# Dividing on GpSimd in slots 4 to 7 and inverting on GpSimd in slots 9 to 23, in a top-k attention kernel with a GELU layer behind it

## The chip, the cores and the metric

One core of a Trainium2 chip runs the whole kernel. It has a matrix engine (TensorE, PE in the profile), a vector engine (VectorE, DVE), an engine for activation functions and copies (ScalarE, ACT), a general engine (GpSimd, POOL), and a queue engine that issues transfers (SyncE, SP). Each works through its own queue of instructions in order, and waits at semaphores for the others. The metric is the device time of one execution in microseconds.

## The reference, cut to what matters

```python
# q, k, v: 8 batches, 8 heads, 576 rows, 64 columns
scores = np.matmul(q, k.transpose(0, 1, 3, 2)) / np.sqrt(64)
kth = np.partition(scores, -32, axis=-1)[..., -32:-31]
scores = np.where(scores >= kth, scores, -1e9)
scores = scores - np.max(scores, axis=-1, keepdims=True)
attn = np.exp(scores)
attn = attn / (np.sum(attn, axis=-1, keepdims=True) + 1e-09)
x = np.matmul(attn, v)        # then (batch, head, row, column) -> 4608 x 512
h = x @ w_in                  # 512 -> 2048
g = h * (1.0 / (1.0 + np.exp(-1.702 * h)))
out = g @ w_out               # 2048 -> 512
```

## The kernel before, in words

The attention is cut into 144 slots. A slot holds 128 rows of query for two heads, or the 64-row ends of two pairs of heads. For each slot the kernel does the following:

- `scores(n)`: TensorE multiplies queries and keys into two banks (`s_ps`). `copy_scores(n)`: ScalarE copies them to a buffer `sc`, of which there are four.
- `pair_up(n)`: VectorE makes the larger and the smaller of each two scores (`ranked`). `topk(n)`: four rounds of MAX8 and three of MATCH_REPLACE8 for each head, on VectorE, give the 32 largest scores (`top`).
- `bounds(n)`: GpSimd makes from them a cut and a bias (`cut`, `low`). `mask(n)` and `exps(n)`: ScalarE drops what is under the cut and takes exponentials (`pr`), with their sums (`den`).
- `invert(n)`: GpSimd adds 1e-9 to the sums (`some`), and VectorE takes the reciprocal (`rden`).
- Then the exponentials are divided by their sums and transposed (`pt`), which goes in two ways. In the first slots, `divide(n)` has GpSimd make two diagonal matrices from `rden`, and `turn_main` and `turn_ends` multiply the exponentials by these on TensorE, which divides and transposes at once; ScalarE copies the result out of the bank. Later, `normalize(n)` divides on GpSimd in place, `split(n)` has ScalarE take the 16-bit halves apart into the buffer `sc` and SyncE write them to memory (`rows`), and `turn_by_dma(n)` brings them back transposed.
- `values`: TensorE multiplies by v, and ScalarE copies the result to its place (`xT`).

Slot n works on the top-k of slot n, and on the exponentials and the division of slot n - 1. The first way is used for the heads of slots 0 to 7, the second from slot 8 on (`BY_DMA = 8`). Besides, in the first slots the weights are loaded and rounded on ScalarE, VectorE and GpSimd (`round_piece`; a shift of each piece is VectorE's). From slot 4 on, TensorE does pieces of the GELU layer (`hidden` and `project`, names `ph`, `unit` and `po`), in each slot and up to the end of the kernel; `tanh` is ScalarE's, `gate` and `combine` are mostly GpSimd's.

What sets the order of the work: slots 0 to 24 (`COLLECTED = 25`) are not issued as they are called. Each step is recorded, and `issue_in_order` issues the steps in the order of the table `ORDER`, which is a list of step numbers; "208+4" means four steps from 208. An engine's queue holds its steps in that order. Slots from 25 on are issued as `joined_pair` writes them, two slots at a time. In the profile, instructions of the table have the line of the recording helper's deferred call, L133, and those of later slots L132.

Of the kernel before, what the change touches and what calls it, by code (L numbers as in the profile page):

```python
# [19 lines left out]
P = 128  # L20
# [125 lines left out]
def kernel(  # L146
# [104 lines left out]


    pieces = [(c, g) for g in range(NG) for c in range(CC)] + [(None, f) for f in range(FC)]
    raw = {}

    def load_piece(n):
        c, g = pieces[n]
# [916 lines left out]
    def slot(n):  # L1174
# [37 lines left out]
        for i, op in enumerate(topk(n)):  # L1212
# [6 lines left out]
            if i == (9 if n < 3 else 7):  # L1219
                if n > BY_DMA:  # L1220
                    invert(n - 1)
                elif n > 0:
                    divide(n - 1)
# [514 lines left out]
```

## Time and profile before

| what | value |
|---|---|
| median of 3 runs | 1342.28 us (1342.17 to 1343.64) |
| the profiled execution | 1342.64 us |
| its span in the profile | 1340.9 us, mean granted TensorE clock 0.996 |
| busy share of the span | PE 99%, PEld 90%, DVE 94%, ACT 86%, POOL 73% |
| DMA | 249.27 MB, mean 186 GB/s |

"Busy" is the time with an instruction of the engine in flight; for PE the ends are modelled, so its share overstates how close it is to its peak. PEld is the loading of the stationary operand, which overlaps with PE. Rows of groups give the busy time, the mean duration of one instruction, and the idle time of the engine before them with what ended it. Rows of the timeline give start and length in microseconds, and in brackets the idle time before, and who ended it. Consecutive instructions of one engine overlap a little in such rows, so the cost of one in a row of them is the distance between starts.

### The profile page before, as it was taken

The numbers are of one execution on the slowest core, as the hardware profiler recorded it, in microseconds if no ns is written. First come the engines' busy times: TensorE is split into PE (matmuls) and PEld (weight loads), VectorE is DVE, ScalarE is ACT, GpSimd is POOL, SyncE is SP. The second block draws the span as 40 slices with busy tenths as digits, with TensorE's granted clock in tenths as the row PEclk, the third lists the DMA queues.
The fourth block names the chain that finished last, engine by engine and source line by source line (L and its number), as shares of the span: only waits on it lengthen the run. The fifth ranks groups of instructions, "written<-read, shape, count | busy, mean of one in ns | idle before, by whom it ended". The sixth has DMA issues, their size and how long they took to land.

```text
span 1340.9 us, 54139 instructions
## 1 busy us (share of the span) xinstructions
PE 1326.5 (99%) x22528; PEld 1202.9 (90%) x22528; DVE 1266.9 (94%) x3371; ACT 1158.4 (86%) x1871; POOL 978.6 (73%) x1788
## 2 busy tenths in 40 slices
PE   8999999999999999999999999999999999999998
PEld 5777689899999999999999999999999999999998
DVE  7999999999999999999999999999999999999902
ACT  6999998999999988999999989899998988888831
POOL 3888987777777777777777777777777777777761
PEclk8999999999999999999999999999999999999999
DMA  7553878888998798989999787988999878755650
GB/s 239 173 169 119 191 182 201 213 191 205 218 219 195 169 206 195 236 191 202 205 220 205 184 188 181 235 199 195 186 228 214 199 158 170 189 140 145 149 116 18
DMA packets 532358, 249.27 MB, mean 186 GB/s; under 512 B 463760, under 2 KB 510352, under 8 KB 532112
## 3 DMA queue, kind: packets, MB, share of 16 engines
q1 hardware_dynamic: 531520, 245.38, 78.5%
q8 instruction: 176, 2.88, 0.9%
q14 instruction: 70, 0.57, 0.1%
q10 hardware_dynamic: 592, 0.43, 0.1%
HBM read 46.01 MB, written 104.60 MB: 112 GB/s over the span
## 4 chain that ended last, share of the span: by engine, by line
PE 94%; DVE 3%; DMA 1%; ACT 1%; SPq 1%; issue 0%; POOL 0%; DVEq 0%; ACTq 0%; POOLq 0%
PE unit L132 32%; PE po L132 29%; PE mixed L132 12%; PE s_ps L132 7%; PE po L133 6%; PE s_ps L133 2%; PE o L133 2%; PE tp L133 2%; PE ph L133 2%; DVE ranked L133 1%; DVE top L133 1%; DMA pt<-rows 1%; ACT sc L133 1%; DMA rows<-sc 0%; SPq L133 0%
## 5 line engine op out<-in xcount | busy, mean ns | idle before, releaser
L132 DVE MAX8 top<-ranked 128x8 f32<-128x288 f32 (+1 forms) x952 | 518.2, 596 | 0.0
L132 PE MATMUL unit<-xT,win 128*64 128x128 f32 x7936 | 454.3, 273 | 0.0
L132 PEld LDWEIGHTS unit<-xT,win 128*64 128x64 f32 x7936 | 437.4, 137 | 0.0
L132 DVE MATCH_REPLACE8 ranked<-top,ranked 128x288 f32<-128x288 f32 x714 | 384.1, 543 | 0.0
L132 PE MATMUL po<-wout,th 128*64 128x128 f32 x4032 | 330.0, 274 | 0.0
L132 POOL TENSOR_TENSOR th<-th,th 128x128 f32<-128x128 f32 x374 | 273.9, 732 | 29.9
L132 PE MATMUL po<-raws,th 128*64 128x128 f32 x3064 | 252.9, 273 | 0.0
L132 PEld LDWEIGHTS po<-wout,th 128*64 128x64 f32 x4032 | 238.3, 137 | 9.9 <-issue 5.1
L132 POOL TENSOR_SCALAR pr<-pr,rden 128x576 f32<-128x576 f32 x240 | 176.5, 745 | 75.2 <-DVE rden L132 75.2
L132 ACT COPY sc<-pr 128x2304 uint16<-128x2304 uint16 x96 | 205.5, 2140 | 1.2 <-POOL pr L132 1.2
L132 PEld LDWEIGHTS po<-raws,th 128*64 128x64 f32 x3064 | 184.6, 137 | 0.0
L132 ACT ACTIVATE th<-unit 128x512 f32<-128x512 f32 x124 | 74.9, 604 | 94.4 <-PE unit L132 94.4
L132 ACT ACTIVATE pr<-sc,low 128x576 f32<-128x576 f32 x192 | 148.1, 786 | 0.0
L132 ACT ACTIVATE sc<-sc,cut 128x576 f32<-128x576 f32 x192 | 140.7, 797 | 0.0
L132 PE MATMUL s_ps<-qk_t 64*64 64x512 f32 x936 | 139.1, 596 | 1.4 <-ACT sc L133 0.8
L132 POOL TENSOR_SCALAR some<-den 128x2 f32<-128x2 f32 x120 | 26.5, 220 | 155.7 <-ACT pr L132 155.4
L132 DVE TENSOR_TENSOR ranked<-s_ps,sc 128x576 f32<-128x576 f32 x188 | 132.8, 748 | 0.0
L132 ACT COPY sc<-s_ps 128x1024 f32<-128x1024 f32 x93 | 95.6, 1028 | 33.8 <-PE s_ps L132 33.7
L132 POOL TENSOR_TENSOR th<-th 128x128 f32<-128x128 f32 x250 | 114.8, 459 | 0.4
L133 DVE MAX8 top<-ranked 128x8 f32<-128x576 f32 (+1 forms) x200 | 111.6, 598 | 0.0
L132 POOL TENSOR_TENSOR raws<-raws 128x128 f32<-128x128 f32 (+1 forms) x160 | 89.7, 569 | 8.1 <-ACT raws L132 3.0
L132 POOL TENSOR_SCALAR th<-th 128x512 f32<-128x512 f32 x124 | 76.5, 617 | 13.1 <-ACT th L132 13.1
(145 smaller groups left out, 2196.6 us busy)
## 6 DMA issues: line engine op xcount, KB each, us to landing
rows<-sc SPq DMA_DIRECT2D x112, 576.0 KB, 3.7
rows<-spare SPq DMA_DIRECT2D x24, 576.0 KB, 3.6
qk_rows<-pr SPq DMA_DIRECT2D x23, 576.0 KB, 4.9
out_dram<-raws SPq DMA_DIRECT2D x66, 128.0 KB, 3.1
raws<-in_moe_w_in_dram SPq DMA_DIRECT2D x16, 512.0 KB, 4.9
raws<-in_moe_w_out_dram SPq DMA_DIRECT2D x16, 512.0 KB, 3.8
qk_l<-in_q_dram SPq DMA_DIRECT2D x28, 256.0 KB, 4.6
qk_l<-in_k_dram SPq DMA_DIRECT2D x28, 256.0 KB, 4.8
```

Of the source, the lines that this page charges most:

```text
L132: return do(*args, **kwargs)
L133: self.engines.collected.append(lambda: do(*args, **kwargs))
```

## The change

Three things change, all in slots 0 to 24.

1. For the heads of slots 4 to 7 the diagonals are no longer made. `slot(n)` calls `invert(n - 1)` in place of `divide(n - 1)` when n is over `TURNS = 4`, and `normalize(n - 1)` divides on GpSimd ahead of `turn_main` and `turn_ends`. Where a slot has no diagonals, `turn` transposes with the identity on TensorE. Eight diagonals leave GpSimd, eight divisions of 128x576 come; on TensorE 32 matmuls with 128 columns and 8 with 64 columns become 36 transposes.
2. In slots 9 to 23 `invert` takes the reciprocal as a power of -1 on GpSimd, from a constant tile that is filled at the start. Fifteen reciprocals leave VectorE. The heads of slots 0 to 8 and those from 24 on keep the reciprocal.
3. The table `ORDER` is new. It is the same up to the step that follows "208+4 130 163 156", and differs from there on to its end. Apart from the steps named above, every engine issues the same instructions as before.

```diff
@@ -37,86 +37,85 @@
 8 11 0+8 9 12 10 13+5 22 18 23+2 33 25 19 26+5 20 31 34 32 21 38+4 35 97 36+2 98 42+8 99 50 54+2 100 56+4 53 51
...
-208+4 130 163 156 213+4 166 157 131 167 159 132 194 191 168 192 212 175 161 171 218 172+3 170 177 158 176 265
...
+208+4 130 163 156 172+3 166 157 131 167 179+3 158 132 171 191 170 213+4 192 194 160 176 212 168 175 178 159 218
...
@@ -252,6 +251,8 @@
     raw = {}
+    minus_one = const.tile([P, 2], F32, name="minus_one")
+    nc.gpsimd.memset(minus_one[:], -1.0)
...
@@ -570,7 +571,10 @@
         rden = st[n]["rden"] = small.tile([P, 2], F32, name="rden", tag="inverse")
-        nc.vector.reciprocal(rden[:], some[:])
+        if BY_DMA < n < COLLECTED - 1:
+            nc.gpsimd.tensor_tensor(out=rden[:], in0=some[:], in1=minus_one[:], op=ALU.pow)
+        else:
+            nc.vector.reciprocal(rden[:], some[:])
...
@@ -595,7 +599,9 @@
             at = (first + c) * P
-            if first != NF:
+            if "by" not in st[n]:
+                nc.tensor.transpose(tp[:, c * P : (c + 1) * P], pr[:, at : at + P], ident[:])
+            elif first != NF:
                 by = st[n]["by"][:, first // NF, :]
...
@@ -1217,7 +1223,7 @@
             if i == (9 if n < 3 else 7):
-                if n > BY_DMA:
+                if n > TURNS:
                     invert(n - 1)
                 elif n > 0:
                     divide(n - 1)
@@ -1249,6 +1255,8 @@
         elif n >= TURNS:
+            if n > TURNS:
+                normalize(n - 1)
             turn_main(n - 1)
             turn_ends(n - 1)
```

157 rows, old and new, of the table ORDER are left out of this document.

## The prediction

> **What bounds the kernel now.** I read the page's first lines, then busy time by stretch, then the chain of waits round the end of slot 24, then VectorE's own idle places. First the page: span, busy time, and the chain that ended last.
>
> ```profile
> span 1340.9 us, 54139 instructions
> PE 1326.5 (99%) x22528; PEld 1202.9 (90%) x22528; DVE 1266.9 (94%) x3371; ACT 1158.4 (86%) x1871; POOL 978.6 (73%) x1788
> PE 94%; DVE 3%; DMA 1%; ACT 1%; SPq 1%; issue 0%; POOL 0%; DVEq 0%; ACTq 0%; POOLq 0%
> ```
>
> TensorE looks like the bound everywhere, but the page itself says that a busy PE is modelled. The change lies in slots 3 to 24, roughly the first 246 us, so I read that part by stretch. Columns: window, length, then busy time of PE, PEld, DVE, ACT, POOL; PEclk; DMA share; GB/s.
>
> ```profile
> 33.00:67.00 34.00, 32.76 (x295) 24.20 (x295) 33.38 (x91) 32.30 (x62) 28.99 (x36) 1.00 0.53 170
> 67.00:110.00 43.00, 42.33 (x365) 31.23 (x360) 41.48 (x110) 40.39 (x82) 36.96 (x50) 1.00 0.44 134
> 110.00:200.00 90.00, 89.86 (x1035) 67.72 (x1029) 89.61 (x239) 87.65 (x146) 80.29 (x114) 1.00 0.71 181
> 200.00:246.00 46.00, 44.58 (x822) 39.68 (x817) 44.89 (x122) 40.97 (x69) 33.83 (x65) 1.00 0.81 194
> 300.00:800.00 500.00, 500.00 (x9080) 466.30 (x9078) 499.34 (x1330) 450.02 (x704) 368.17 (x707) 1.00 0.89 202
> ```
>
> From 33 to 246 us VectorE is idle for 0.62 + 1.52 + 0.39 + 1.11 = 3.64 us in all. Weight loading fills 71 to 87% of those stretches against 93% later, so PE is not at its peak there, while VectorE cannot go faster than its list of top-k steps. The chain at the end of slot 24 agrees (start, length, what):
>
> ```profile
> 244.37 1.85 DVE ranked L132 x4
> 246.22 0.04 issue
> 246.27 1.09 PE s_ps L132 x8
> ...
> 247.57 3.21 PE po L132 x56
> ```
>
> Up to 246 us the last thing waited for is VectorE; from there PE runs without a gap almost to the end (500.00 busy of 500 us). PE's work behind that point is the same in both kernels, so a microsecond that VectorE gains before 246 us is a microsecond off the end, and a microsecond of PE work saved before it is worth something only where VectorE waited for PE.
>
> **The change, part by part.**
>
> *Reciprocals off VectorE, slots 9 to 23.* Fifteen leave. Their recorded 0.15 us overlaps the next instruction, so I take start to start:
>
> ```profile
> 119.41 0.16 DVE L133 RECIPROCAL rden<-some 128x2 f32<-128x2 f32 x1
> 119.49 1.40 DVE L133 MAX8 top<-ranked 128x8 f32<-128x576 f32 x2
> 129.44 0.15 DVE L133 RECIPROCAL rden<-some 128x2 f32<-128x2 f32 x1
> 129.50 0.74 DVE L133 MAX8 top<-ranked 128x8 f32<-128x576 f32 x1
> ```
>
> That is 0.08 and 0.06, so 15 x 0.07 = 1.05 us, all on the bounding engine. VectorE's places of idle time that matter here (in brackets the idle time before, and who ended it):
>
> ```profile
> 81.27 0.76 DVE L133 TENSOR_TENSOR ranked<-s_ps,sc 128x576 f32<-128x576 f32 x1 [0.19 <-PE s_ps L133]
> 101.77 0.76 DVE L133 TENSOR_TENSOR ranked<-s_ps,sc 128x576 f32<-128x576 f32 x1 [0.95 <-PE s_ps L133]
> 110.39 0.76 DVE L133 TENSOR_TENSOR ranked<-s_ps,sc 128x576 f32<-128x576 f32 x1 [0.40 <-PE s_ps L133]
> 225.29 0.17 DVE L133 RECIPROCAL rden<-some 128x2 f32<-128x2 f32 x1 [0.25 <-POOL some L133]
> 227.10 0.76 DVE L133 TENSOR_TENSOR ranked<-s_ps,sc 128x576 f32<-128x576 f32 x1 [0.86 <-ACT sc L133]
> ```
>
> One moved reciprocal stood waiting for GpSimd, in order ahead of top-k steps: 0.25 us, which goes too.
>
> *Plain transposes, heads of slots 4 to 7.* Eight 128-wide matmuls per head become transposes, and two half-wide ones become one.
>
> ```profile
> 103.62 1.95 PE L133 MATMUL tp<-xT,pr 128*128 128x128 f32 x16
> 105.40 0.59 PE L133 MATMUL po<-wout,th 128*128 128x512 f32 x1
> ...
> 148.81 0.60 PE L133 MATMUL tp<-ident,raws 128*128 128x128 f32 x4
> 149.25 1.02 PE L133 MATMUL po<-wout,th 128*128 128x512 f32 x2
> ```
>
> Start to start, eight matmuls (16 records) take 1.78 us and four transposes 0.44, so eight take 0.88: 0.90 saved per head. The block of the ends took this long in the chain:
>
> ```profile
> 106.43 0.37 PE tp L133 x4
> ```
>
> It becomes one transpose of 0.11: up to 0.26 more, and nothing if its two halves already overlap with other work. Four heads: 3.6 to 4.6 us, I take 4.0. PE has slack there, so none of this counts by itself. What counts is the three waits on score matmuls, 0.19 + 0.95 + 0.40 = 1.54 us, in slots 8, 10 and 11, at and behind the heads that are saved. Adding these durations along PE's queue in the two issue orders, the last score matmul of slots 8, 10 and 11 comes 10.4, 2.4 and 4.9 us of PE work earlier in the new one, and those of slots 12 to 24 come 1.3 to 6.0 earlier. I count the 1.54 us as gone; bounds 0 and 1.54.
>
> *GpSimd: what is added.* These are the groups of the first 270 us (xcount | busy, mean ns | idle):
>
> ```profile
> L133 POOL TENSOR_SCALAR pr<-pr,rden 128x576 f32<-128x576 f32 x32 | 23.7, 749 | 4.0 <-DVE rden L133 3.8
> L133 POOL TENSOR_TENSOR th<-th,th 128x512 f32<-128x512 f32 x10 | 12.8, 1278 | 0.2
> L133 POOL TENSOR_SCALAR xT<-ident,rden 128x128 f32<-128x128 f32 x16 | 5.9, 373 | 0.5
> L133 POOL TENSOR_TENSOR low<-cut 128x2 f32<-128x2 f32 x25 | 4.9, 194 | 0.6
> ```
>
> Eight divisions of 0.749 come, eight diagonals of 0.373 go: +3.0 us. GpSimd idles 6.04 us between 67 and 110, so they are covered; the transposes now wait 0.75 us longer per head for their data, and behind them in PE's queue stand the score matmuls, whose lead pays it. Fifteen powers come, an operation that no row shows. Its bounds are the 128x2 tensor_tensor (0.194) and the 128x512 one (1.28): 2.9 to 19.2 us in all. It has the small one's shape, so I take 0.19. GpSimd idles 9.71 + 12.17 = 21.9 us between 110 and 246, so either end is hidden in the sum. On the path of one slot the power replaces a wait of 3.8 / 7 = 0.54 us (the division's row above: seven waits for the reciprocal), so it breaks even there at 0.54. The memset of the constant is one small instruction at the start: nothing, since GpSimd waits there for the first top-k.
>
> *The new table.* It keeps the sequence of the first 170 or so steps and changes the rest. Added along the queues with the same durations, the pairings of VectorE lie up to 2.8 us later among its own steps, and the ScalarE copies that they need move by similar amounts, so that their lead changes by under a microsecond in most slots; it shrinks by 0.8 in slot 24, where VectorE waits already (0.86 above). Bounds: the idle time of VectorE left over from the two items above, 3.64 - 1.54 - 0.25 = 1.85 us, may go entirely, or one more wait as long as a scores-buffer transfer may come (4.57 us, below). I take no change.
>
> *What hides the rest, and what comes next.* ScalarE must follow VectorE. At the end of slot 24 its sums come late:
>
> ```profile
> 247.31 0.22 POOL L132 TENSOR_SCALAR some<-den 128x2 f32<-128x2 f32 x1 [3.08 <-ACT pr L132]
> ...
> 248.17 0.16 DVE L132 RECIPROCAL rden<-some 128x2 f32<-128x2 f32 x1
> ```
>
> This reciprocal stays on VectorE, with a lead of 248.17 - 247.53 = 0.64 us. If VectorE comes 2.84 us earlier and ScalarE doesn't, VectorE waits 2.2 us here. For ScalarE's coming along speak 5.03 idle us of it between 200 and 246, and that its waits in the opening are mostly for PE, which now leads by 4 us:
>
> ```profile
> ACT pt L133 <- PE tp L133: 2.6, 6, 0.8
> ACT xT L133 <- PE o L133: 2.2, 4, 1.6
> ```
>
> *Sum.* 1.05 + 0.25 + 1.54 = 2.84 us. The profiled execution took 1342.64 us, 1.7 more than its span and 0.36 more than the median of 1342.28; the difference carries over, so 1342.28 - 2.84 = **1339.4 us**.
>
> [...] In the stretch of 110 to 200 us, which holds the transposes quoted at 148.81, the granted clock is 1.00. [...] I give it 0.04.
>
> **Rivals.**
>
> *ScalarE sets the pace instead.* Place: the reciprocal at 248.17. VectorE keeps the 0.64 us of lead, the rest is waited away: 1342.28 - 0.64 = 1341.6. For it: ScalarE's 87.65 of 90 us busy from 110 to 200. Against: its waits for PE. Chance 0.21.
>
> *The power is dear: slower.* Place: GpSimd's queue from slot 10 on, where the division of the same head and the bounds of the next slots stand behind it. It decides from 21.9 / 15 = 1.46 us each. At 2 us it adds 15 x 0.54 = 8.1 us beyond GpSimd's idle time, and PE's waits are off: 1342.28 - 2.84 + 8.1 = 1347.5. For it: no row shows a power on GpSimd. Against: two elements per partition, and 0.19 for a sum of that size. Chance 0.12. [...]
>
> *The table brings one more wait for a buffer.* The pairing at 227.10 waited for this chain:
>
> ```profile
> 221.76 4.57 DMA rows<-sc
> ...
> 226.43 0.65 ACT sc L133
> ...
> 227.10 1.19 DVE ranked L133 x2
> ```
>
> A copy of scores needs the buffer whose transfer out is still running. One such full wait more: 1339.4 + 4.57 = 1344.0; two: 1348.5. For it: slot 24's lead shrinks. Against: divisions no longer wait for VectorE. Chance 0.14.
>
> **How the numbers follow.** Forecast 0.49, between 1337.6 (all 3.64 us of idle and the 1.05 go) and 1340.5 (half of PE's waits and the 0.25 stay); ScalarE 0.21; power 0.12; buffer 0.14; clock 0.04. The range leaves out the power and the case of two buffer waits, and reaches a little past both ends that are left: 1337.3 to 1345.0. Changes of 0.2%, 2.7 us, are about what a measurement of this kernel can tell from none. Faster than that, below 1339.6: five sixths of the forecast, 0.41. Slower, above 1345.0: the power, and half of the buffer case (more than one full wait): 0.19. Within: 0.40.
>
> **What would show it.** In the changed profile: VectorE's pairings of slots 8, 10 and 11 without a PE wait; eight transposes near 0.9 us per head; powers near 0.2 us; the chain handing over from VectorE to PE near 243.4 us instead of 246.27, with PE full behind it. Wrong would be: powers above 1.4 us, VectorE waiting for sums near the end of slot 24, new waits on copies of scores in slots 13 to 24, or a clock below 1.00 between 67 and 110 us.

## The result, and the profile after

The change made the kernel slower: 1345.50 us (1344.99 to 1348.61) against 1342.62 us (1341.62 to 1343.85) beside it, medians of 11 runs each, a ratio of 1.0021 with a 95% interval of 1.0013 to 1.0028. It is 2.9 us more, where 2.8 us less were forecast. The profiled execution took 1347.45 us, 2 us above that median, so its own difference to the profile of before (4.8 us) is larger than the typical one. Of these 4.8 us 0.97 are there at VectorE's first pairing (10.23 us against 9.26), where both kernels still issue the same order; in four kernels of the experiments, which have that order up to there too (`old_pow`, `old_both`, `new_none`, `old_plain`), that pairing begins at 9.34 to 9.92 us. At least a part of that share, then, is not the change's.

First the page of the changed kernel: span, busy time, and the engines in the chain that ended last. (Here the table's instructions have line L132 and those of later slots L131; in the kernels of the experiments these lines shift by a few.)

```profile
span 1345.7 us, 54053 instructions
PE 1327.3 (99%) x22484; PEld 1202.2 (89%) x22484; DVE 1268.6 (94%) x3356; ACT 1158.6 (86%) x1871; POOL 993.5 (74%) x1804
PE 82%; DMA 1%; ACT 0%; SPq 0%; issue 0%; DVE 0%; DVEq 0%
```

VectorE's 3% of the chain have gone to 0%: it is no longer VectorE that ends the table's part. The same stretches as before (busy PE, PEld, DVE, ACT, POOL, then the granted clock, DMA share, GB/s):

```profile
33.00:67.00 34.00, 29.72 (x239) 21.97 (x238) 32.68 (x88) 29.32 (x57) 28.04 (x38) 0.89 0.49 164
67.00:110.00 43.00, 41.78 (x332) 28.86 (x330) 41.74 (x109) 40.43 (x81) 36.97 (x46) 1.00 0.40 127
110.00:200.00 90.00, 90.00 (x970) 66.09 (x970) 89.60 (x234) 87.82 (x152) 85.08 (x121) 1.00 0.70 180
200.00:246.00 46.00, 44.62 (x846) 40.23 (x846) 44.23 (x112) 40.55 (x64) 42.29 (x76) 1.00 0.84 189
300.00:800.00 500.00, 499.47 (x9068) 465.53 (x9066) 498.70 (x1327) 449.75 (x704) 367.53 (x706) 1.00 0.90 201
```

Three things are to be seen. From 33 to 67 us, ahead of nearly all that was edited, TensorE is busy for 29.72 us instead of 32.76, at a mean clock of 0.89 instead of 1.00. From 110 to 246 us GpSimd has 13.3 us more to do (127.37 against 114.12). And the steady part from 300 us on is what it was. The first of these, in TensorE's timeline (in brackets the idle time before, and who ended it):

```profile
37.41 0.70 PE L132 MATMUL s_ps<-qk_t 64*64 64x288 f32 x2 [1.42 <-DVE ranked L132]
...
46.22 1.39 PE L132 MATMUL tp<-xT,pr 128*128 128x128 f32 x8 [2.10 <-POOL xT L132]
```

TensorE stands 2.10 us for the diagonals of an early head. In GpSimd's timeline these diagonals come behind 2.55 us of weight pieces that the new table puts ahead of them:

```profile
43.11 2.55 POOL L132 TENSOR_TENSOR win<-win,raws 128x512 int32<-128x512 int32 x2
45.61 0.20 POOL L132 TENSOR_TENSOR low<-cut 128x2 f32<-128x2 f32 x1
45.79 0.73 POOL L132 TENSOR_SCALAR xT<-ident,rden 128x128 f32<-128x128 f32 x2
```

Behind that gap the granted clock is 0.50 for six microseconds:

```profile
44.00:47.00 3.00, 0.90 (x9) 0.79 (x8) 2.97 (x10) 3.00 (x5) 3.00 (x6) 1.00 0.74 265
47.00:53.00 6.00, 5.55 (x32) 4.73 (x34) 6.00 (x17) 4.73 (x11) 4.29 (x5) 0.50 0.48 155
```

GpSimd's groups of the first 270 us (xcount | busy, mean ns | idle):

```profile
L132 POOL TENSOR_SCALAR pr<-pr,rden 128x576 f32<-128x576 f32 x40 | 29.9, 752 | 0.9 <-PE tp L132 0.3
...
L132 POOL TENSOR_TENSOR rden<-some,minus_one 128x2 f32<-128x2 f32 x15 | 11.0, 736 | 0.2
...
L132 POOL TENSOR_TENSOR low<-cut 128x2 f32<-128x2 f32 x25 | 5.5, 219 | 0.4
```

A power of two elements per partition takes 0.736 us on average, not 0.19. Then VectorE's waits from 90 us on:

```profile
94.77 0.76 DVE L132 TENSOR_TENSOR ranked<-s_ps,sc 128x576 f32<-128x576 f32 x1 [0.65 <-ACT sc L132]
125.66 1.42 DVE L132 TENSOR_TENSOR ranked<-s_ps,sc 128x576 f32<-128x576 f32 x2 [0.40 <-ACT sc L132]
...
223.70 0.76 DVE L132 TENSOR_TENSOR ranked<-s_ps,sc 128x576 f32<-128x576 f32 x1 [0.36 <-ACT sc L132]
232.42 0.76 DVE L132 TENSOR_TENSOR ranked<-s_ps,sc 128x576 f32<-128x576 f32 x1 [0.72 <-ACT sc L132]
243.70 1.42 DVE L132 TENSOR_TENSOR ranked<-s_ps,sc 128x576 f32<-128x576 f32 x2 [0.56 <-ACT sc L132]
```

No pairing waits for TensorE's score matmuls any more, as forecast; they wait for ScalarE's copies (`sc`) instead, which stood among the prediction's signs of being wrong. Last the chain of waits where the table's part ends (start, length, what):

```profile
216.49 3.85 DMA rows<-sc
220.33 0.02 issue
220.35 9.38 DMA pt<-rows
229.73 0.14 issue
229.86 2.60 PE o L132 x80
...
248.61 1.53 PE po L132 x28
...
252.25 2.76 PE po L131 x47
```

TensorE takes over from a transfer at 229.86 and works without a gap through the point that was 247.57 before and is 252.25 now. Of the 4.8 us 4.7 are there by then. What comes last ahead of that stretch is no longer VectorE, but two transfers behind a copy of ScalarE's.

### The profile page after: what moved, and what is told of

The parts are those of the page before. It is cut to its first block, busy times and chain, and to the rows that moved or that the text cites. A ratio compares the mean times of both kernels' runs of the same rounds, so it can differ in the third digit from the quotient of the medians.

```text
span 1345.7 us, 54053 instructions
## 1 busy us (share of the span) xinstructions
PE 1327.3 (99%) x22484; PEld 1202.2 (89%) x22484; DVE 1268.6 (94%) x3356; ACT 1158.6 (86%) x1871; POOL 993.5 (74%) x1804
## 4 chain that ended last, share of the span: by engine, by line
PE 82%; DMA 1%; ACT 0%; SPq 0%; issue 0%; DVE 0%; DVEq 0%
PE unit L131 32%; PE po L131 29%; PE mixed L131 12%; PE s_ps L131 7%; DMA pt<-rows 1%; PE ph L132 1%; PE po L132 0%; PE o L132 0%; DMA rows<-sc 0%; ACT sc L132 0%; PE s_ps L132 0%; SPq L131 0%; DVE raws L131 0%; ACT pr L132 0%; ACT th L131 0%
## 5 line engine op out<-in xcount | busy, mean ns | idle before, releaser
L131 DVE MAX8 top<-ranked 128x8 f32<-128x288 f32 (+1 forms) x952 | 518.5, 597 | 0.0
L131 PE MATMUL unit<-xT,win 128*64 128x128 f32 x7936 | 454.2, 273 | 0.0
L131 PEld LDWEIGHTS unit<-xT,win 128*64 128x64 f32 x7936 | 437.4, 137 | 0.0
L131 DVE MATCH_REPLACE8 ranked<-top,ranked 128x288 f32<-128x288 f32 x714 | 384.5, 544 | 0.0
L131 PE MATMUL po<-wout,th 128*64 128x128 f32 x4032 | 329.8, 274 | 0.0
L131 POOL TENSOR_TENSOR th<-th,th 128x128 f32<-128x128 f32 x374 | 274.3, 733 | 29.9
L131 PE MATMUL po<-raws,th 128*64 128x128 f32 x3064 | 252.8, 273 | 0.0
L131 PEld LDWEIGHTS po<-wout,th 128*64 128x64 f32 x4032 | 238.1, 137 | 9.9 <-issue 5.3
L131 POOL TENSOR_SCALAR pr<-pr,rden 128x576 f32<-128x576 f32 x240 | 177.3, 750 | 74.0 <-DVE rden L131 74.0
L131 ACT COPY sc<-pr 128x2304 uint16<-128x2304 uint16 x96 | 205.5, 2141 | 1.0 <-POOL pr L131 0.9
L131 PEld LDWEIGHTS po<-raws,th 128*64 128x64 f32 x3064 | 184.5, 137 | 0.0
L131 ACT ACTIVATE th<-unit 128x512 f32<-128x512 f32 x124 | 74.9, 604 | 94.5 <-PE unit L131 94.5
L131 ACT ACTIVATE pr<-sc,low 128x576 f32<-128x576 f32 x192 | 148.1, 786 | 0.0
L131 POOL TENSOR_SCALAR some<-den 128x2 f32<-128x2 f32 x120 | 26.6, 222 | 157.0 <-ACT pr L131 156.4
L131 ACT ACTIVATE sc<-sc,cut 128x576 f32<-128x576 f32 x192 | 140.8, 797 | 0.1
L131 PE MATMUL s_ps<-qk_t 64*64 64x512 f32 x936 | 139.0, 596 | 0.0
L131 DVE TENSOR_TENSOR ranked<-s_ps,sc 128x576 f32<-128x576 f32 x188 | 132.8, 749 | 0.4 <-ACT sc L132 0.4
L131 ACT COPY sc<-s_ps 128x1024 f32<-128x1024 f32 x93 | 95.6, 1028 | 33.8 <-PE s_ps L131 33.7
L131 POOL TENSOR_TENSOR th<-th 128x128 f32<-128x128 f32 x250 | 115.1, 460 | 0.4
L132 DVE MAX8 top<-ranked 128x8 f32<-128x288 f32 (+1 forms) x200 | 111.0, 595 | 0.0
L131 POOL TENSOR_TENSOR raws<-raws 128x128 f32<-128x128 f32 (+1 forms) x160 | 89.9, 571 | 8.1 <-ACT raws L131 3.0
L131 POOL TENSOR_SCALAR th<-th 128x512 f32<-128x512 f32 x124 | 77.4, 624 | 13.1 <-ACT th L131 13.1
```

The lines of the kernel that those rows point to most:

```text
L131: return do(*args, **kwargs)
L132: self.engines.collected.append(lambda: do(*args, **kwargs))
```

## The experiments

The change has three parts: the powers, the divisions with plain transposes, and the table. Four kernels were made first, to take them apart. A table for a program that lacks an edit is the other table's sequence, with the steps that the edit replaces standing where their replacements stood. The theories: T, the table itself is the loss; P, the power is; L, the later transposes are (they wait for divisions instead of diagonals). The kernels ran in several rounds, on three chips, and the median of before lay between 1342.62 and 1344.74 us; so each kernel is compared with the runs of before beside it, by a ratio with its 95% interval, and two kernels by the difference of their ratios (0.0010 is 1.34 us).

*The new table alone* (`new_none`): the code of before, with the order of the changed kernel.

> The new table alone, without either edit: each reciprocal stands on VectorE at the place of its power, each diagonal at the place of a division, and the second half of a block of ends right behind the first. Theory T (the table is the loss, through waits in slots 2 to 9): 3 to 5 us slower than before, with the VectorE waits for copies of scores in the first 100 us as in the changed kernel. Theory P (the power is the loss): within 1 us of before. Theory L (the later transposes are the loss): within 1 us of before.

Measured: 1349.70 us, ratio 1.0037 [1.0023, 1.0051]. Without either edit the new order costs 5 us, as theory T had it. TensorE's gap of 2.10 us stands there too, and so does the fall of the clock behind it, with no plain transpose in the program:

```profile
45.80 1.44 PE L127 MATMUL tp<-xT,pr 128*128 128x128 f32 x6 [2.10 <-POOL xT L127]
```

```profile
43.00:46.00 3.00, 0.90 (x11) 0.39 (x4) 3.00 (x7) 3.00 (x4) 3.00 (x5) 1.00 0.75 248
46.00:50.00 4.00, 3.55 (x21) 2.96 (x21) 3.97 (x13) 2.76 (x7) 2.43 (x4) 0.57 0.61 213
```

*The powers alone, in the old order* (`old_pow`):

```diff
-        nc.vector.reciprocal(rden[:], some[:])
+        if BY_DMA < n < COLLECTED - 1:
+            nc.gpsimd.tensor_tensor(out=rden[:], in0=some[:], in1=minus_one[:], op=ALU.pow)
+        else:
+            nc.vector.reciprocal(rden[:], some[:])
```

> The power alone with the old table. Theory T: 0 to 1.3 us faster than before. Theory P (0.72 us each on GpSimd, 10.8 us in all, hold up the divisions and the bounds behind them): 2 to 4 us slower. Theory L: 0 to 1.3 us faster.

Measured: 1348.06 us, ratio 1.0025 [1.0016, 1.0034], 3.3 us slower. In its profile everything stands within 0.1 us of before until slot 11; then VectorE falls behind, 1.3 us by slot 15 and 3.8 by slot 24, in waits such as these:

```profile
168.75 0.76 DVE L128 TENSOR_TENSOR ranked<-s_ps,sc 128x576 f32<-128x576 f32 x1 [1.00 <-ACT sc L128]
...
230.89 0.76 DVE L128 TENSOR_TENSOR ranked<-s_ps,sc 128x576 f32<-128x576 f32 x1 [1.82 <-ACT sc L128]
```

ScalarE's copies come late because ScalarE stands waiting at an earlier step of its queue. Its waits between 110 and 246 us (us in total, times, longest), before and with the powers:

```profile
ACT sc L133 <- POOL pr L133: 1.4, 4, 0.6
```

```profile
ACT sc L128 <- POOL pr L128: 5.3, 9, 1.2
```

`split` copies the divided exponentials, the division stands behind the power on GpSimd, and the next slot's score copy stands behind `split` on ScalarE. So ScalarE waited for a division nine times in this stretch, against four before, although GpSimd was idle for 13.3 of its 136 us.

*The divisions and plain transposes alone, in the old order* (`old_plain`):

```diff
-                if n > BY_DMA:
+                if n > TURNS:
                     invert(n - 1)
...
+            if n > TURNS:
+                normalize(n - 1)
```

> Divisions and plain transposes in slots 5 to 8 alone, with the old table. Theory T: 0 to 2 us faster than before. Theory P: 0 to 2 us faster. Theory L (the transposes wait for the divisions): 2 to 4 us slower.

Measured: 1344.95 us, ratio 1.0005 [0.9993, 1.0017]. Four microseconds less of TensorE's work bring nothing that can be told in the old order. In three of its twelve runs the mean granted clock is under 0.995, which none of the 29 runs of before beside it shows, and these three took 1346.9 to 1350.2 us. The profiled execution is one of them: the shorter transposes leave a longer gap (0.68 us before), and behind it the clock falls.

```profile
73.21 1.15 PE L128 MATMUL tp<-ident,pr 128*128 128x128 f32 x8
75.75 0.43 PE L128 MATMUL o<-pt,v_l 128*64 128x128 f32 x2 [1.39 <-ACT pt L128]
```

```profile
77.00:83.00 6.00, 6.00 (x26) 4.25 (x25) 5.50 (x15) 6.00 (x14) 5.76 (x6) 0.51 0.98 248
```

*Both edits, in the old order* (`old_both`): the two diffs above together.

> Both edits with the old table: each power at the place of its reciprocal, each division at the place of a diagonal. Theory T: 1 to 3 us faster than before (the 1.05 us of reciprocals and part of the 1.54 us of waits for PE, less what the longer steps on GpSimd cost). Theory P: 2 to 4 us slower. Theory L: 2 to 4 us slower.

Measured: 1348.44 us, ratio 1.0032 [1.0020, 1.0043]. So the new order, which costs 5 us by itself, takes some 1.5 us back once both edits are there (1.0021 against 1.0032; the intervals overlap). L falls: by `old_plain` the later transposes cost nothing that can be told. T and P hold in part, and the parts don't add up. The next kernels were for that.

*The new order with divisions and transposes, without powers* (`new_plain`): the changed kernel with `nc.vector.reciprocal(rden[:], some[:])` in all slots.

> The changed kernel with its table, its divisions and its plain transposes; the fifteen inversions go back to VectorE as reciprocals, at the places that the powers have in the table. If the power of 0.72 us on GpSimd still costs in the new table what it costs in the old one (3.3 us for the powers alone), this is 2 to 3 us faster than the changed kernel: ratio to before 0.9995 to 1.0005. If the new table hides the powers, the fifteen reciprocals (1.05 us) come back for nothing and the waits for GpSimd with them: ratio 1.0020 to 1.0035. With the diagonals too the new table alone took 1.0037; the plain transposes in it should then be worth 1 to 2 us.

*The changed kernel with a product in place of the power* (`new_times`), *and the old order with that product* (`old_times`); both leave out the inversion, and keep all else:

```diff
-            nc.gpsimd.tensor_tensor(out=rden[:], in0=some[:], in1=minus_one[:], op=ALU.pow)
+            nc.gpsimd.tensor_tensor(out=rden[:], in0=some[:], in1=minus_one[:], op=ALU.mult)
```

> The changed kernel with the power replaced by a product of the same two tiles on GpSimd (128x2, the inverse is left out, so that the division multiplies by minus the sum). It should take the 0.19 to 0.22 us that I had put down for the power, and all else, the order too, is the changed kernel's. If the mis-sized power is a loss of the changed kernel: 1.5 to 3 us faster than it, ratio to before 0.9995 to 1.0010. If the new table hides the power's length: within 0.5 us of the changed kernel, ratio 1.0018 to 1.0025.

> The old table with the inversions of slots 9 to 23 on GpSimd as a product (the inverse is left out) in place of the power; diagonals and matmuls as before. If the 3.3 us that the powers alone cost in the old table come from their length of 0.72 us, this one is before less 1.05 (reciprocals) and less up to 0.25 (one wait): ratio 0.9990 to 0.9995. If they come from the place in GpSimd's queue and not from the length, the ratio stays at 1.0020 to 1.0025.

Measured: `new_plain` 1346.29 us, ratio 1.0017 [1.0008, 1.0025]; `new_times` 1346.61, 1.0018 [1.0009, 1.0027]; `old_times` 1344.59, 1.0006 [0.9998, 1.0015]. The product took what I had put down for the power:

```profile
L128 POOL TENSOR_TENSOR rden<-some,minus_one 128x2 f32<-128x2 f32 x15 | 2.9, 196 | 0.5
```

In the old order the power's length is 2.6 of its 3.3 us (1.0025 against 1.0006). In the changed kernel it is worth 0.4 us, within the intervals: with the plain transposes there, the new order hides most of it. `new_plain` fell between its two ranges, and `old_times` missed both of its own. It is the change as I had priced it, fifteen reciprocals off VectorE for 0.2 us each on GpSimd, and it isn't faster than before. Its VectorE waits show where the 1.05 us went:

```profile
174.89 0.76 DVE L128 TENSOR_TENSOR ranked<-s_ps,sc 128x576 f32<-128x576 f32 x1 [0.32 <-ACT sc L128]
...
228.41 0.76 DVE L128 TENSOR_TENSOR ranked<-s_ps,sc 128x576 f32<-128x576 f32 x1 [1.62 <-ACT sc L128]
258.71 0.17 DVE L127 RECIPROCAL rden<-some 128x2 f32<-128x2 f32 x1 [0.45 <-POOL some L127]
```

Before, the wait at the same pairing was 0.86 us (227.10), and the other two were none. In the trace of before, ScalarE's copies end 0.16 to 0.92 us ahead of VectorE's pairing in ten of the slots 12 to 23; here five of these have no lead left. VectorE ran into them. ScalarE's own waits for divisions hardly grew (1.8 us in all, against 1.4 before), which speaks for ScalarE's pace, and against the move to GpSimd, as what took the gain.

*Old order first, new order behind* (`old_then_new`): both edits; the old order up to VectorE's first step of slot 9 (the seam), then the remaining steps in the new one.

> Both edits; the steps stand in the old table's order up to VectorE's first step of slot 9, and in the new table's order behind it. If the new table's loss lies in slots 2 to 8 (in the profiles VectorE falls 2.8 us behind in slots 3 to 6, and 3.2 by slot 9, the later start aside), this is about 3 us faster than the changed kernel: ratio to before 0.9990 to 1.0005. If the loss comes from the order behind slot 9, or is made good there by the early order, the ratio is 1.0020 or more.

Measured: 1345.43 us, ratio 1.0016 [1.0006, 1.0027]. It fell between its two ranges and didn't tell: the old order brought its gap of 1.41 us behind the plain transposes of 73 us along, and the clock fell there, as in `old_plain` (0.50 from 78 to 83 us), and once more behind a gap of 2.12 us that ends at 99.67 (0.50 from 101 to 104). So the seam was moved ahead of these transposes.

*The same with the seam at slot 5* (`early_old5`), *and the changed kernel on the same chip* (`after_again`).

> Both edits; the steps stand in the old table's order up to VectorE's first step of slot 5 and in the new table's order behind it. Theory G (the new table lets TensorE idle 2.10 us at 44 us, behind GpSimd's late diagonals, and the granted clock falls to half for some 4 to 7 us): with the old order there the gap is 0.81 us as before, the clock stays at 1.00 from 33 us on, and the kernel is 2 to 3 us faster than the changed one: ratio to before 0.9993 to 1.0005. Rival B (the loss lies behind slot 9, where ScalarE has no lead on VectorE): ratio 1.0015 or more. With the new order behind slot 5 the gap of 1.4 us at 74 us that the old order had together with plain transposes should not be there either.

> The changed kernel once more, on the same chip as the three others, as their base: ratio 1.0013 to 1.0028 as measured, a gap of TensorE of about 2.1 us near 44 us and a clock of 0.5 for some microseconds behind it in the profile.

Measured: `early_old5` 1344.81 us, 1.0015 [1.0006, 1.0024]; `after_again` 1346.00, 1.0022 [1.0013, 1.0031]. The gap at 44 us and the low clock are gone with the old order, but the time lies where rival B had put it (1.0015 or more), and not where theory G had (at most 1.0005):

```profile
33.00:67.00 34.00, 30.10 (x245) 21.24 (x244) 33.93 (x91) 31.08 (x60) 30.66 (x39) 1.00 0.51 165
67.00:110.00 43.00, 42.53 (x351) 29.55 (x353) 42.10 (x109) 40.50 (x82) 36.85 (x45) 1.00 0.44 134
110.00:200.00 90.00, 90.00 (x986) 66.07 (x983) 89.60 (x235) 86.93 (x148) 85.70 (x123) 1.00 0.68 177
200.00:246.00 46.00, 46.00 (x870) 42.12 (x866) 45.52 (x116) 42.55 (x69) 41.21 (x75) 1.00 0.93 207
```

That is worth 1.2 us by the medians; the intervals overlap, so the size is loose. In the profile of `after_again` the clock fell in another place (0.50 from 38 to 44 us), behind a gap of 2.54 us at 35 us: in the first profile of this kernel the gap of over 2 us was the one at 44 us, in this one that at 35. The last two rows are the news: from 110 to 246 us TensorE has no idle time left, and the chain of waits in this profile is TensorE's queue alone from 76 us into slot 25. That suggests that with the new order TensorE sets the time there. The changed kernel is like this from 110 to 200 us (90.00 of 90); from 213 to 230 us its chain runs through ScalarE and two transfers, for which TensorE stands 1.11 us, and so does that of `early5_times` below from 210 to 226.

*Matmuls with the identity in place of plain transposes*, in the old order without powers (`old_matmul`), and in the kernel with the seam at slot 5 (`early5_matmul`). This gives TensorE its 0.9 us per head back and leaves GpSimd as it is:

```diff
-                nc.tensor.transpose(tp[:, c * P : (c + 1) * P], pr[:, at : at + P], ident[:])
+                nc.tensor.matmul(tp[:, c * P : (c + 1) * P], lhsT=pr[:, at : at + P], rhs=ident[:])
```

> The old table with the divisions of slots 4 to 7 on GpSimd, transposed by matmuls with the identity instead of plain transposes, so that TensorE keeps its 1.78 us per head; reciprocals on VectorE as before. Theory G: the gap of TensorE at 74 us goes back from 1.39 us to about 0.6, no run shows a mean clock under 0.995 (with plain transposes 3 of 12 did), and the spread is that of before: median ratio 0.9998 to 1.0004, highest run under 1347 us. If the plain transposes gave anything by themselves, it is slower than with them (1.0005), at 1.0010 or more.

> Both edits with powers, the old order up to slot 5 and the new one behind it; the heads of slots 4 to 7 are transposed by matmuls with the identity, which costs TensorE some 0.9 us more per head. If TensorE sets the pace in the new order, this is 2.5 to 4 us slower than with plain transposes: ratio 1.0033 to 1.0045. If not, within 0.5 us of it: 1.0012 to 1.0019. In the old order the same swap made no difference (1.0004 against 1.0005).

Measured: `old_matmul` 1343.52 us, 1.0004 [0.9995, 1.0013], against 1.0005 with plain transposes, and its highest run is 1345.26; `early5_matmul` 1350.04 (5 runs), 1.0047 [1.0033, 1.0061], against 1.0015. The same 4 us of TensorE's work are worth nothing in the old order and 4.3 us in the new one: in the new order TensorE's work counts at about its full length.

*The new order and powers, without plain transposes* (`new_pow`): `turn`, `divide` and `slot` as before the change.

> The changed kernel without its plain transposes: diagonals and matmuls in slots 4 to 7 as before, the powers and the new table. The new table alone took 1.0037, with the plain transposes 1.0017, with both edits 1.0021. If the plain transposes are what makes the new table tolerable (its order counts on 4 us less of TensorE), this one stays at 1.0035 to 1.0045. If the powers do it, 1.0015 to 1.0025.

Measured: 1351.44 us (5 runs), 1.0059 [1.0047, 1.0072], more than expected. It points the same way: in the new order with powers the divisions and plain transposes are worth 5 us, and without powers 2.7 (1.0037 against 1.0017). In its profile TensorE also stands 2.29 us at 234 us, and the clock falls behind that (0.50 from 236 to 238), which isn't in the others. And without the plain transposes the new order doesn't hide the power: it costs 3.0 us there (1.0059 against 1.0037, intervals that just overlap).

*Product* (`early5_times`) *and reciprocals on VectorE* (`early5_plain`) in place of the powers, in the kernel with the seam at slot 5.

> Both edits, the old order up to slot 5 and the new one behind it, with the power replaced by a product on GpSimd (the inverse is left out). If the power's length of 0.72 us is what is left of the loss: 1 to 2 us faster than with the power (1.0015), ratio 1.0000 to 1.0007. If TensorE sets the pace in the new order, GpSimd's 0.5 us per slot do not matter: 1.0012 to 1.0017.

> As before it, with VectorE's reciprocals at the places of the powers; plain transposes and divisions stay. If the move of the inversions to GpSimd is what is left of the loss: ratio 0.9997 to 1.0005. If VectorE's 1.05 us count: 1.0018 to 1.0025. If TensorE sets the pace: 1.0010 to 1.0017, like the two others.

Measured: `early5_times` 1344.93 us, 1.0010 [1.0001, 1.0019]; `early5_plain` 1345.81, 1.0019 [1.0010, 1.0027]; with the power it was 1.0015. The power's length is worth some 0.7 us there, within the intervals; that lies between the two ranges of `early5_times`. Taking the inversions back to VectorE doesn't help. All ratios in one table, each against before:

| order | neither edit | powers | divisions and transposes | both |
|---|---|---|---|---|
| old | 1 | 1.0025 | 1.0005 | 1.0032 |
| new | 1.0037 | 1.0059 | 1.0017 | 1.0021 |
| old up to slot 5, then new | not tried | not tried | 1.0019 | 1.0015 |

No kernel beat the one before.

## Why the prediction was wrong

The sum was 2.84 us of VectorE's time, and the table nothing. Both of its parts were tried by themselves in the old order. The reciprocals and the one wait behind them (1.05 + 0.25) should have given 0.9990, and `old_times` measured 1.0006 [0.9998, 1.0015]; the waits for score matmuls (1.54) should have given 0.9989, and `old_plain` measured 1.0005 [0.9993, 1.0017] (its nine runs without the low clock have a median of 1344.21 us, 0.5 under that of before, a third of what was forecast). So the step that failed first is the reading of the bound in point 3, then the power's price and place in points 1 and 2, and the table in point 6.

1. *"I take 0.19" for the power.* It measured 0.736 us, inside the bounds of 0.194 and 1.28 but far from the end that I took. I chose by shape; the product of the same two tiles took 0.196 (`old_times`), so it was the operation that decided here.

2. *"It decides from 21.9 / 15 = 1.46 us each."* This step was worse than the price. I had worked out both thresholds, 0.54 us on the path of one slot and 1.46 us over GpSimd's idle time, and let the second one count ("either end is hidden in the sum"). With the powers alone in the old order it failed: at 0.72 us, half of 1.46, the power cost 3.3 us, 2.6 of them by its length, with GpSimd idle for 13.3 us in the same stretch. That idle time didn't cover a step that another engine waited for: ScalarE's waits for divisions grew from 1.4 to 5.3 us. The rival "the power is dear" had the sign right, but not its 1347.5 us, and in the changed kernel the power's length is worth only 0.4 to 0.7 us.

3. *1.05 us of reciprocals, "all on the bounding engine".* They left VectorE's queue. With a cheap operation in their place the kernel got no faster (`old_times`, 1.0006). VectorE was never idle for long, and that is why I called it the bound; but ScalarE's copies followed it so closely that its gain became waits. I looked for ScalarE's lead in one place only, the reciprocal at 248.17; this was the mechanism of the rival "ScalarE sets the pace", which got 0.21, though it shows at the score copies of slots 18 to 24 and not at that reciprocal. The sentence "up to 246 us the last thing waited for is VectorE" was read from the chain's end alone. Further back the chain of before is TensorE's. From 98 to 112 us, and then from 160 to 232 (shares of each stretch):

```profile
by line: PE po L133 41.5%; PE s_ps L133 21.7%; PE tp L133 18.9%; PE o L133 18.1%
by line: PE po L133 27.1%; PE ph L133 18.5%; DMA pt<-rows 9.1%; PE s_ps L133 8.3%; ACT sc L133 6.7%; PE o L133 6.6%; DMA rows<-sc 6.3%; SPq L133 5.5%; DVE ranked L133 3.7%; DVE top L133 3.3%; PE tp L133 2.2%; issue 2.1%; ACT spare L133 0.9%
```

From 33 to 246 us VectorE stands in it only from 227.10 on. With VectorE idle for 0.39 of the 90 us from 110 to 200 besides, and TensorE for 0.14, several queues ran with next to no idle time at once, and time taken from one of them alone brought nothing: neither TensorE's 4 us (`old_plain`) nor VectorE's 1 us (`old_times`). No kernel took both from the old order without the power's length, so that this would have paid isn't shown.

4. *Plain transposes, 4.0 us of TensorE's work.* Size right. Eight of them take 0.90 us from start to start (77.10 to 78.00), where 0.88 was worked out:

```profile
77.10 1.06 PE L132 MATMUL tp<-ident,pr 128*128 128x128 f32 x8 [0.47 <-ACT xT L132]
78.00 1.06 PE L132 MATMUL po<-xT,win 128*128 128x128 f32 x8
```

5. *The three waits for score matmuls and the one at 225.29, 1.54 + 0.25 us.* They are gone in the changed kernel, as forecast. It didn't matter, since VectorE no longer ended the chain. That TensorE's work "is worth something only where VectorE waited for PE" doesn't hold in the new order: there 4 us of it were worth 4.3 (`early5_matmul`), with weight loading at 73% (66.07 of 90 us in `early_old5`), no more than the 75% of before (67.72) that I had read as "not at its peak".

6. *The new table, "I take no change".* It has no price of its own: it costs 5 us with neither edit, and with both it takes some 1.5 back. So the sum fails either way round, by the edits in the old order (4.3 us slower by the ratio instead of 2.84 faster) or by the table without them. I compared the leads of slot after slot by adding durations along the queues and saw moves of under a microsecond; I didn't look at the diagonals of the first slots, where GpSimd's order leaves TensorE idle for 2.10 us at 44 us (in `after_again` the large gap, of 2.54 us, is the one at 35), nor at the clock behind such a gap (0.50 from 47 to 53 us). The early part is worth about 1.2 us, within the intervals.

7. *The clock, 0.04.* No run shows four heads of plain transposes at half clock: in the changed kernel they begin between 77.10 and 109.5 us, and the clock was 1.00 from 67 to 110. But the clock did fall, behind gaps, in the new order from 33 to 67 us (0.89 on average in the changed kernel) and in the old order with plain transposes at 77 us (0.51 from 77 to 83).

The 2.9 us, then: about 1.2 us is the early order with its gap and clock, 0.4 to 0.7 the length of the power, and the rest, a good microsecond, remains without powers and without the early order (`early5_times`, 1.0010 [1.0001, 1.0019]). The first two lie within the intervals, and the last is barely clear of them. Where the rest comes from stays open. From 33 to 110 us TensorE is idle for 4.37 us in `early_old5` and `early5_times` (77 less 30.10 and 42.53) against 1.91 before, which may be it, but was not tried; and in the profile of `early5_times` the pairing that VectorE begins at 262.06 us before the change comes only 0.79 us later, while the first pairing of all comes 0.83 later.

## What to carry to other kernels

When an operation moves to another engine, ask in each round who waits for it there: here a queue with a sixth of its time idle (21.9 of 136 us) didn't hide a step that stands ahead of what the next engine needs now. An engine that hardly idles need not be the bound (VectorE, idle for 0.39 of 90 us here, gained nothing from 1.05 us less of work in `old_times`); look whether the others have a lead on it, read the lead at every hand-over, not at one, and follow the chain of waits back through the whole part that changes, not only from its end. A hand-written order and the edits that it was written for are one change: a part alone can cost more than the whole (the order 5.0 us, the powers 3.3, all together 2.9).

## What the runs showed of the hardware

A power of 128x2 on GpSimd took 0.736 us on average in the changed kernel, the product of the same two tiles 0.196 in `old_times`. The first power of the changed kernel, at 122.72 us, took 0.74; its fifteen lie between 0.708 and 0.952 us.

The granted clock mostly fell behind TensorE's longer gaps. Between 33 and 240 us, in the profiles of these kernels, every idle gap of 2.1 us or more (eight of them, 2.10 to 2.55) had 3.4 or 6.8 us at a clock of 0.50 behind it, and none of 1.0 to 1.8 us did, but for those of 1.4 us that came right behind eight plain transposes: two of these three did (`old_plain` and `old_then_new`, 6.8 us each). Ahead of 33 us at least one gap went against it, so no sharp line is shown: in `new_times` one of 1.79 us, ending at 30.77, had 3.4 us at 0.50 behind it. What part the transposes have in it isn't shown either: in `old_plain` there are 1.15 us of them ahead of a gap of 1.39 us, and `old_both`, with the same transposes and a gap of 1.41 us at 75 us, kept a clock of 1.00.
